# Two spectral layers and two convolution layers on one core: when the rows of the second layer are made, how its norms are split, and which buffers it loads into

## The chip, the cores and the metric

One core of a Trainium2 chip runs the whole program in one launch. The metric is device time in microseconds (us): the median of the runs shown. The engines are named as in the profile: PE is TensorE (matrix products), PEld its weight loads, DVE is VectorE, ACT is ScalarE, POOL is GpSimd, SP is SyncE, which here only issues DMAs.

## The reference, cut to what matters

The input x has 2048 rows (the sequence) of 576 elements (the hidden dimension), in float32. Four sublayers follow each other, each added to its input; the third and fourth repeat the first two.

```python
x = x + A(layernorm(x))      # layer 1
x = x + B(layernorm(x), ...)
x = x + A(layernorm(x))      # layer 2
x = x + B(layernorm(x), ...)

# A: real part of a DFT over the hidden dimension and over the sequence
a = einsum("bsd,ed->bse", x, dft_hid_re)
b = einsum("bsd,ed->bse", x, dft_hid_im)
y = einsum("ts,bse->bte", dft_seq_re, a) - einsum("ts,bse->bte", dft_seq_im, b)

# B: a gate; everything beside x comes from k, v and the kernels, not from x
kv = causal_conv4(k, shift_k) * v
y = causal_long_conv(kv, ssm_k) + kv * ssm_D      # by FFT, length 2 * 2048
return x * y
```

The long convolution does not depend on x. The kernel computes it once and uses it for both B sublayers.

## The kernel before, in words

**Products.** Every float32 matrix is cut in two parts of reduced precision, "high" and "low" (`split`, lines 84 to 86: ACT copies the high part, DVE subtracts it to get the low part), and a product is three matmuls: high·high, high·low, low·high. A matmul moves 512 columns in the sequence products and 288 columns in all others.

**Layer 1 and the first block of layer 2** are run by `layer` (lines 277 to 315). The 2048 output positions are four blocks `tb`; for each block and each of the cosine and the sine matrix (`g`) there are 16 steps `k`, one for each chunk of 128 positions. In a step PE multiplies row chunk X[k] (the normalized row, kept in `xs`, both parts) by one tile of the sequence matrix `c_mat` into four PSUM banks `s` and one bank `rm` for the last 64 columns: 14 matmuls of 512 columns. The tile of `c_mat` (256 KB) is loaded two steps ahead into one of `CRAW` raw tiles and split into one of three `cs` tiles (`load_c`, lines 186 to 193). After 16 steps the banks are moved into the tile `u` (`evac_u`, `evac_r`). Layer 1 has 128 steps (n = 0 to 127), the first block of layer 2 has 32. The generator yields twice in a step, and the code around it puts other work there.

**The hidden DFT** of a finished block (`hidden`, lines 252 to 266) works on `u` and on the matrix W: 27 matmuls of 288 columns make one half of one row chunk, called a piece here. `finish(pending, n)` emits n pieces. In layer 1 pieces of one block are spread over steps of the next; the last block of layer 1 is finished in the first steps of layer 2, one piece a step, so that row 12 of layer 1's output is complete after step 2 of layer 2, row 13 after step 4, row 14 after step 6 and row 15 after step 8 (line 830).

**W** is loaded by `load_w` (lines 200 to 225) in nine chunks through the ring of raw tiles `wl`: three chunks after each of the steps 41, 42 and 43 (lines 608 to 610). The `wl` tiles lie over tiles that the branch used before: the first four over `so` (results on their way to memory), the next two over `v`, the last over `tmp`.

**The branch** (the long convolution, `branch`, lines 324 to 522) is a generator. Its first part (16-point and 128-point transforms of kv and the kernel, "f1") takes 33 calls of `next(br)` and ends at step 40 (F1_END). Its second part ("mid" and "i2") lays out its tiles, loads the constants `mc` on POOL's queue and its first two inputs from the DRAM tensor `t` (lines 495 and 496), splits them and goes on in units of `mid_forward`, `mid_inverse` and `i2_products`, paced by `spent` from step 44 (W_END + 1) on (lines 611 to 620). In the kernel before, all of that begins with the first paced call at step 44, after the nine loads of W.

**Norms.** `normed` (lines 165 to 169) and `normed_x` (lines 532 to 542) normalize a row chunk: statistics, then a power by POOL (`L162`, `L539`), then one small DVE operation and one ACT pass that use it. In layer 1 `get_x0` (line 551) does this for row j up to XLEAD = 3 steps ahead of its use, and `to_x` (lines 171 to 176) puts both parts into `xs`.

**Rows of layer 2.** `get_x1` (lines 562 to 572) loads a row chunk `xa` of layer 1's output and the gate `yb`, makes the gated row (`gated`, lines 524 to 530), stores it (`xb`, line 569), normalizes it, stores that (`y`, line 571) and puts it into `xs`. Its tiles are six `xa`, six `yb` and two `xj`. In the kernel before it is called for rows 0 to 11 after each of the steps 113 to 124 of layer 1 (PREP = 113, lines 625 to 630), and for rows 12 to 15 by `layer` itself, at the start of steps 9 to 12 of layer 2, three steps ahead of use (lines 285 to 287).

**The other three blocks of layer 2** are computed by one level of Strassen's scheme (`strassen`, lines 768 to 824): seven products m in the order 5, 1, 6, 2, 7, 3, 4, each in four steps `kp` of two halves. A step has 12 matmuls of 512 columns, and 16 in the products 5, 1, 2 and 4, which also fill a bank for the last 64 columns. `load_step` (lines 716 to 730) loads 512 KB of `c_mat` a tile: two tiles a step for products 5 and 7, one for 1, 2 and 4, none for 6 and 3. Raw tiles come from the ring `cw` (three tiles, one in `flts`, two in `ph`) or `csum`. `ahead(n + 4, ...)` emits loads four steps ahead. The last-columns bank of the sine side is `rm`, that of the cosine side one of the three banks `b` (`bank()`); `store_r` (lines 697 to 702) moves it out at the end of products 2 and 4. The tiles are laid out at step 14 of layer 2 (STATIC, lines 831 to 844): `save`, `both` and `post` share the rest of `ph`.

**Order.** The code emits work in the order written; the framework then gives each engine and each DMA queue one fixed order, by a priority that follows the order of emission and by its own estimate of when an instruction can start, so an engine's order is not exactly that of the code. On the chip each engine and each queue runs its order in sequence.

Of the kernel before, what the change touches and what calls it, by code (L numbers as in the profile page):

```python
# [10 lines left out]
F32 = mybir.dt.float32  # L11
# [13 lines left out]
EPS = 1e-5  # L25
ASTAT = 8
XLEAD = 3
K_FIRST = 2
F1_16 = 4
F1_END = 40  # L30
# [28 lines left out]
def fnet_h3_kernel(ctx: ExitStack, tc: tile.TileContext, x, c_mat, w_re, w_im, k_pad, v, shift_k,  # L59
# [51 lines left out]
    def lay(t, at, *sizes):  # L111

        for name, words, n in sizes:
            ring.setdefault(name, Ring()).tiles.extend(t[:, at + i * words:at + (i + 1) * words] for i in range(n))
            at += n * words
        assert at <= t.shape[1], (at, t.shape, sizes)
        return at
# [46 lines left out]

    def normed(src, y):
        mv, rs, nb = norm_stats(src)
        nc.vector.tensor_scalar(nb, mv[:, 0:1], rs, -1.0, op0=OP.mult, op1=OP.mult)
        nc.scalar.activation(y, src, AF.Identity, bias=nb, scale=rs)
        return y

    def to_x(y, j):
        t = xs[:, j, :]
# [27 lines left out]
    W = []  # L200

    def load_w():
        lay(flts, SC_AT + CRAW * NT, ("wl", D, 7))
        wg = region_a(FR, "w").rearrange("p (k n) -> p k n", k=9)
        for ch in range(9):
            w = two(wg[:, ch])
            raw = ring["wl"]()
            if ch < 8:
                nc.sync.dma_start(raw, (w_re if ch < 4 else w_im)[(ch % 4) * P:(ch % 4 + 1) * P, :])
            else:  # L210
                nc.sync.dma_start(raw[:REM], w_re[NC * P:, :])
                nc.sync.dma_start(raw[REM:], w_im[NC * P:, :])
            for lo, hi, sg in ((0, P, 1 if ch < 4 else -1),) if ch < 8 else ((0, REM, 1), (REM, P, -1)):
                if sg > 0:
                    split(w[lo:hi, 0, :], w[lo:hi, 1, :], raw[lo:hi])
                else:
                    nc.scalar.activation(w[lo:hi, 0, :], raw[lo:hi], AF.Copy, scale=-1.0)
                    nc.vector.scalar_tensor_tensor(w[lo:hi, 1, :], raw[lo:hi], -1.0,
                                                   w[lo:hi, 0, :].bitcast(F32), op0=OP.mult,
                                                   op1=OP.subtract)  # L220
            W.append(w)
            yield
        for ch in range(9):
            load_after(w_d[ch], wg[:, ch].bitcast(F32))
            yield
# [51 lines left out]
    def layer(get_x, xres, done, pending, blocks=TB):  # L277
        steps = [(g, tb, k) for tb in range(blocks) for g in range(2) for k in range(J)]
        for n, (g, tb, k) in enumerate(steps):
            for i in range(2):  # L280
                if n == 0 and steps[i] not in CT:
                    load_c(steps[i])
            if n + 2 < len(steps):
                load_c(steps[n + 2])
            for i in range(XLEAD + 1):
                if n + i < J:
                    get_x(n + i)
            if k == 0:
                ps = list(acc4)
                ps.append(psp.tile([P, NT], F32, tag="rm", name="rm"))  # L290
            c = CT.pop(steps[n])
            first, last = k == 0, k == J - 1
            if last and g == 0:
                finish(pending, 99)
            for dc in range(NC):
                xh = X[k][:, dc * P:(dc + 1) * P]
                xl = X[k][:, D + REM + dc * P:D + REM + (dc + 1) * P]
                mm(ps[dc], xh, c[0], first, False)
                mm(ps[dc], xh, c[1], False, False)
                mm(ps[dc], xl, c[0], False, last)  # L300
                if dc == NC // 2 - 1:
                    yield n, False
                if last:
                    (evac_u if blocks == TB else save_u)(g, ps, dc)
            xr = X[k][:, NC * P:D + REM]
            mm(ps[NC], xr, c[0], first, False)
            mm(ps[NC], xr, c[1], False, last)
            if last and blocks < TB:
                store_r(tb, g, ps[NC])
            elif last:  # L310
                evac_r(g, ps)
                if g == 1:
                    us = dict(U)
                    pending.extend([us, tb, jj, xres, done] for jj in range(TB))
            yield n, True
# [8 lines left out]
    def branch():  # L324
# [170 lines left out]

        load_feed(0)
        load_feed(1)
        split_feed(0)
        for i, (kind, hf, q) in enumerate(feeds):
            df, fc = halves.pop(i)  # L500
# [31 lines left out]
    def normed_x(src, y, junk):  # L532
        m = ring["stat"]()
        sm, sv, rs, nb = (m[:, i:i + 1] for i in range(4))
        nc.scalar.activation(junk, src, AF.Copy, accum_out=sm)
        nc.vector.tensor_scalar(sm, sm, -1.0 / D, None, op0=OP.mult)
        nc.scalar.activation(junk, src, AF.Square, bias=sm, accum_out=sv)
        nc.vector.tensor_scalar(sv, sv, 1.0 / D, EPS, op0=OP.mult, op1=OP.add)
        pows.append(nc.gpsimd.tensor_tensor(rs, sv, mhalf, OP.pow).ins)  # L539
        nc.vector.tensor_tensor(nb, sm, rs, OP.mult)  # L540
        nc.scalar.activation(y, src, AF.Identity, bias=nb, scale=rs)
        return y

    XL = {}

    def load_x(j):
        if j < J:
            XL[j] = ring["x"]()
            nc.sync.dma_start(XL[j], x[:, j, :])

    def get_x0(j):
        if X[j] is None:
            load_x(j + 2)
            src = XL.pop(j)
            X[j] = to_x(normed_x(src, src, ring["junk"]()) if j >= ASTAT else normed(src, src), j)

    def done0(j, xa):
        nc.sync.dma_start(xa_d[j], xa)
# [3 lines left out]
    def get_x1(j):  # L562
        if j in ready:
            return
        ready.add(j)
        xa = ring["xa"]()
        load_after(xa, xa_d[j])
        xb = gated(xa, j, True)
        nc.sync.dma_start(xb_d[j], xb)
        y = normed_x(xb, xa, ring["xj"]())  # L570
        stored.append(nc.sync.dma_start(y_d[j // 2][:, j % 2, :], y).ins)
        X[j] = to_x(y, j)

# [26 lines left out]
    for n, whole in layer(get_x0, lambda j: x[:, j, :], done0, pending):  # L600
        if whole and n <= F1_END:
            want = K_FIRST + (F1_16 * n // 16 if n <= 16 else F1_16 + (32 - K_FIRST - F1_16) * (n - 16) // (F1_END - 16))
            while used < want:
                next(br)
                used += 1
            if n == F1_END:
                next(br)
        if whole and F1_END < n <= W_END:
            for _ in range(3):
                next(wl, 0)  # L610
        if n > W_END:
            if whole and pieces(n):
                finish(pending, 1)
            m = n - W_END - 1
            if m + 1 < len(paced):
                done_by = paced[m] + (paced[m + 1] - paced[m] if whole else STEP * 3 / 7)
            else:
                done_by = total
            while spent < work * done_by / total:
                spent += next(br, work)  # L620
        if not whole:
            continue
        if n >= W_SAVE and n % 2 == 0:
            next(wl, 0)
        m = n - PREP
        if m == 0:
            lay(flts, SC_AT + CRAW * NT + 2 * D, ("xa", D, 2), ("yb", D, 2))
            lay(region_b(F32, "gate"), 0, ("xa", D, 4), ("yb", D, 4), ("xj", D, 2))
        if 0 <= m < TB * (TB - 1):
            get_x1(m)  # L630
    T, R, t7 = {}, {}, []

    def t_slot(m, kp):
# [134 lines left out]
    def strassen():  # L768
        acc, rem = {}, {}
        for n, (tb, m, kp) in enumerate(steps):  # L770
            if kp == 0:
                acc[m] = pair(m, acc)
                if m in (5, 1):
                    g = REMS[m][0]
                    rem[g] = psp.tile([P, NT], F32, tag="rm", name="rm") if g else bank()
            for i in range(2):
                ahead(n + 4, 2 * n + i + CSB)
                c = cs.pop(2 * n + i)
# [48 lines left out]
    for n, whole in layer(get_x1, lambda j: xb_d[j], done1, pending, 1):  # L827
        if not whole:
            continue
        finish(pending, 1)  # L830
        if n == STATIC:
            anchor.append(stored[-1])
            t7.append(region_a(FR, "t7"))
            ph = region_b(F32, "ph")
            fresh("craw", "rems")
            lay(flts, SC_AT, ("rems", 2 * REM, 2), ("csum", WIDE, 4), ("cw", WIDE, 1))
            at = lay(ph, 0, ("cw", WIDE, 2))
            lay(ph, at, ("save", NT, 8))
            lay(ph, at, ("both", WIDE, 2), ("post", WIDE, 2))
            ring["craw"].tiles.extend(c[:, :NT] for c in ring["cw"].tiles)  # L840
            old = ring.pop("cs")
            free, *held = (old() for _ in range(3))
            lay(t7[0], 7 * WIDE + 16 * REM, ("cs", WIDE, 2))
            ring["cs"].tiles.extend([free, *held])
# [104 lines left out]
```

## Time and profile before

| | |
|---|---|
| median of 3 runs (lowest to highest) | 1245.86 us (1243.02 to 1246.0) |
| profiled execution, device time | 1238.42 us |
| span of that execution (first to last instruction) | 1236.6 us |
| mean granted TensorE clock | 0.992 of full speed |
| PE busy | 1192.3 us (96%), 6320 matmuls |
| DVE busy / ACT busy / POOL busy | 847.0 / 657.1 / 80.9 us |
| DMA traffic | 261.97 MB, mean 212 GB/s |

A row of the windows view gives a stretch, its length, then for each engine the busy time and the number of instructions in it, the granted clock of TensorE, the busy share of the DMA engines and GB/s. A row of the chain of waits gives start, length and what the chain ran through. A row of the timeline gives start, length, engine, line, operation, output<-inputs, shapes, a count, and in brackets how long the engine had been idle and what ended that. A row of the groups view gives line, engine, operation, tiles, shapes and count, then busy time and mean duration in ns, then idle time before. PE's busy time uses modelled ends of the matmuls. All times inside the span are counted from its start.

### The profile page before, as it was taken

Reading aid. Unit: us, or ns where it says so; the run is one execution under the profiler, and the core shown is the slowest. Engines: PE = TensorE matmul, PEld = TensorE weight load, DVE = VectorE, ACT = ScalarE, POOL = GpSimd, SP = SyncE. Lnnn points to the kernel's source line nnn. Section 1 sums busy time; section 2 is a strip of 40 time slices with the busy share of each in tenths; the row PEclk is TensorE's granted clock in tenths of the full one; section 3 lists DMA queues with packets and bytes.
Section 4 is the critical chain, followed back from the end, with each engine's and each line's share of the span. In section 5 each row is a group of like instructions: output and inputs, shape, how many; then the busy total and the mean of one; then the engine's idle time right before and its main releaser. Section 6 shows DMA issues by size and latency. Waiting matters only on the chain.

```text
span 1236.6 us, 18361 instructions
## 1 busy us (share of the span) xinstructions
PE 1192.3 (96%) x6320; PEld 1033.2 (84%) x6320; DVE 847.0 (68%) x1559; ACT 657.1 (53%) x1315; POOL 80.9 (7%) x116
## 2 busy tenths in 40 slices
PE   7999998999999999999999998999999999999997
PEld 6778887987888888898987797888778787789997
DVE  7999983759786677775368615676676667674674
ACT  7955665659776667765457614544344344460220
POOL 1210000000000000001113102000000000000111
PEclk9999999999999999999999999999999999999999
DMA  8989988536656656566968635882673678776631
GB/s 303 306 256 305 292 266 254 183 109 172 193 192 209 195 180 192 181 190 198 327 222 271 228 95 189 267 280 77 191 268 95 180 254 266 230 266 222 207 127 40
DMA packets 145968, 261.97 MB, mean 212 GB/s; under 512 B 15825, under 2 KB 44497, under 8 KB 145874
## 3 DMA queue, kind: packets, MB, share of 16 engines
q1 hardware_dynamic: 102674, 205.73, 52.2%
q10 hardware_dynamic: 36288, 42.48, 9.9%
q0 software_dynamic: 6912, 12.59, 4.0%
q8 instruction: 50, 0.82, 0.3%
q14 instruction: 44, 0.36, 0.1%
HBM read 194.09 MB, written 66.65 MB: 211 GB/s over the span
## 4 chain that ended last, share of the span: by engine, by line
PE 70%; DVE 10%; DMA 10%; ACT 5%; issue 3%; POOL 1%; SPq 0%; ACTq 0%; POOLq 0%; DVEq 0%
PE s L68 36%; PE bk L68 28%; PE rm L68 6%; DMA ph<-in_c_mat 2%; DMA flts<-in_c_mat 2%; DVE mats L86 2%; ACT mats L85 1%; POOL flts L539 1%; DVE ph L725 1%; DMA gate<-xa 1%; DVE mats L176 1%; DMA xb<-gate 1%; DMA flts<-t 1%; POOL flts L162 1%; DVE f1f L383 1%
## 5 line engine op out<-in xcount | busy, mean ns | idle before, releaser
L68 PE MATMUL s<-mats 128*128 128x512 f32 x2094 | 532.3, 395 | 13.5 <-DVE u L86 6.5
L68 PEld LDWEIGHTS s<-mats 128*128 128x128 f32 x2094 | 388.0, 190 | 89.4 <-DVE u L86 7.6
L85 ACT ACTIVATE mats<-flts 128x512 fp32r<-128x512 f32 x209 | 130.9, 627 | 147.8 <-PE rm L68 101.3
L86 DVE TENSOR_TENSOR mats<-flts,mats 128x512 fp32r<-128x512 f32 x209 | 143.3, 688 | 67.3 <-ACT mats L85 65.0
L68 PE MATMUL bk<-mid 128*128 128x288 f32 x768 | 128.2, 301 | 7.3 <-ACT mid L85 4.1
L68 PEld LDWEIGHTS bk<-mid 128*128 128x128 f32 x768 | 113.3, 188 | 25.1 <-ACT mid L85 8.2
L86 DVE TENSOR_TENSOR mid<-flts,mid 128x576 fp32r<-128x576 f32 (+1 forms) x160 | 100.4, 637 | 33.9 <-ACT mid L85 30.6
L68 PEld LDWEIGHTS bk<-w,u 128*128 128x128 f32 x864 | 119.2, 190 | 3.7 <-ACT flts L452 1.3
L68 PE MATMUL bk<-w,u 128*128 128x288 f32 x864 | 121.3, 297 | 0.9 <-ACT flts L452 0.9
L85 ACT ACTIVATE mid<-flts 128x576 fp32r<-128x576 f32 (+1 forms) x160 | 92.5, 586 | 37.2 <-DVE flts L441 29.6
L68 PE MATMUL rm<-mats 128*128 128x512 f32 x338 | 105.5, 392 | 2.6 <-DVE flts L701 1.7
L68 PEld LDWEIGHTS rm<-mats 128*128 128x128 f32 x338 | 63.5, 189 | 17.0 <-DVE flts L701 2.1
L162 POOL TENSOR_TENSOR flts<-flts 128x1 f32<-128x1 f32 x40 | 36.8, 921 | 559.6 <-DVE flts L161 554.9
L264 DVE TENSOR_TENSOR flts<-flts,bk 128x288 f32<-128x288 f32 x48 | 21.7, 452 | 69.0 <-PE bk L68 68.8
L68 PE MATMUL bk<-f1r 128*128 128x288 f32 x384 | 60.6, 300 | 7.7 <-ACT f1r L85 6.4
L68 PEld LDWEIGHTS bk<-f1r 128*128 128x128 f32 x384 | 57.1, 192 | 12.2 <-ACT f1r L85 6.4
L68 PE MATMUL s<-t,mats 128*128 128x512 f32 x258 | 64.3, 389 | 0.0
L68 PEld LDWEIGHTS s<-t,mats 128*128 128x128 f32 x258 | 48.4, 188 | 10.1
L68 PE MATMUL bk<-mats 128*128 128x288 f32 (+1 forms) x340 | 56.8, 309 | 0.0
L398 ACT ACTIVATE flts<-bk 128x288 f32<-128x288 f32 x128 | 48.5, 410 | 14.7 <-PE bk L68 12.6
L438 DVE TENSOR_TENSOR flts<-bk,flts 128x288 f32<-128x288 f32 x64 | 29.1, 455 | 32.7 <-ACT flts L434 32.4
L68 PEld LDWEIGHTS bk<-mats 128*128 128x128 f32 x340 | 48.8, 188 | 2.0
(148 smaller groups left out, 1559.8 us busy)
## 6 DMA issues: line engine op xcount, KB each, us to landing
flts<-in_c_mat SPq DMA_DIRECT2D x150, 256.0 KB, 3.5
ph<-in_c_mat SPq DMA_DIRECT2D x48, 512.0 KB, 3.9
t<-flts ACTq DMA_DIRECT2D x64, 288.0 KB, 4.5
flts<-t SPq DMA_DIRECT2D x64, 288.0 KB, 3.4
flts<-in_c_mat SPq DMA_DIRECT2D x36, 512.0 KB, 5.0
vd<-flts ACTq DMA_DIRECT2D x64, 144.0 KB, 3.0
flts<-vd SPq DMA_DIRECT2D x32, 288.0 KB, 4.1
mid<-in_i2c POOLq DMA_DIRECT2D x32, 256.0 KB, 4.4
```

The source lines that it names most:

```text
L68: nc.tensor.matmul(ps, lhsT, rhs, start=first, stop=last, skip_group_check=more)
L85: nc.scalar.activation(h, src, AF.Copy)
L86: nc.vector.tensor_tensor(l, src, h.bitcast(F32), OP.subtract)
L162: pows.append(nc.gpsimd.tensor_tensor(rs, ve, mhalf, OP.pow).ins)
L176: nc.vector.tensor_tensor(t[:, D + REM:], y[:, :NC * P], h[:, :NC * P], OP.subtract)
L264: nc.vector.tensor_tensor(r[:, cs], r[:, cs], ps[:, :HD], OP.add)
L383: nc.vector.tensor_tensor(r, r, tmp, OP.add)
L398: nc.scalar.activation(so[:, c, :], ps[:, :HD], AF.Copy)
L438: nc.vector.tensor_tensor(p1, px[:, :HD], p1, OP.mult)
L539: pows.append(nc.gpsimd.tensor_tensor(rs, sv, mhalf, OP.pow).ins)
L725: nc.vector.tensor_tensor(src, src, r, OP.add)
```

## The change

1. Rows of layer 2: during layer 1, `get_x1` is called for rows 0 to 7 only, after every second step from 113 to 127. Rows 8 to 15 are made in layer 2, after the steps 0, 1, 2, 3, 4, 5, 7 and 9 (`ROWS`). In the first block of layer 2, `layer` no longer looks three steps ahead (by then each row has been asked for).
2. The loads of the branch's second part: `load_w` gets four raw tiles (over `so`) in place of seven, and the second part of the branch yields once right after its first two loads. It is called for that after step 42, behind the sixth chunk of W; its paced calls begin at step 44 as before.
3. Norms in two steps: `normed` and `normed_x` yield after the power. In layer 1 the statistics and the power of row j + 1 are emitted before the rest of row j (`stats0`). In layer 2 both halves of a norm still follow each other.
4. Strassen's raw tiles: the ring `cw` has four tiles in place of three, `save` six in place of eight, `post` one in place of two.
5. Banks: the last-columns bank of both sides is one of the three banks `b`; `rm` is no longer used there.

```diff
+ROWS = (0, 1, 2, 3, 4, 5, 7, 9)
...
     def normed(src, y):
         mv, rs, nb = norm_stats(src)
+        yield
         nc.vector.tensor_scalar(nb, mv[:, 0:1], rs, -1.0, op0=OP.mult, op1=OP.mult)
         nc.scalar.activation(y, src, AF.Identity, bias=nb, scale=rs)
-        return y
...
-        lay(flts, SC_AT + CRAW * NT, ("wl", D, 7))
+        lay(flts, SC_AT + CRAW * NT, ("wl", D, 4))
...
-            for i in range(XLEAD + 1):
+            for i in range(XLEAD + 1 if blocks == TB else 1):
                 if n + i < J:
                     get_x(n + i)
...
         load_feed(0)
         load_feed(1)
+        yield 0
         split_feed(0)
...
         pows.append(nc.gpsimd.tensor_tensor(rs, sv, mhalf, OP.pow).ins)
+        yield
         nc.vector.tensor_tensor(nb, sm, rs, OP.mult)
         nc.scalar.activation(y, src, AF.Identity, bias=nb, scale=rs)
-        return y
-
-    XL = {}
+
+    XL, LN = {}, {}
...
+    def stats0(j):
+        if j < J and j not in LN:
+            src = XL.pop(j)
+            LN[j] = src, normed_x(src, src, ring["junk"]()) if j >= ASTAT else normed(src, src)
+            next(LN[j][1])
+
     def get_x0(j):
         if X[j] is None:
             load_x(j + 2)
-            src = XL.pop(j)
-            X[j] = to_x(normed_x(src, src, ring["junk"]()) if j >= ASTAT else normed(src, src), j)
+            stats0(j)
+            if j > 0:
+                stats0(j + 1)
+            src, ln = LN[j]
+            next(ln, 0)
+            X[j] = to_x(src, j)
...
-        y = normed_x(xb, xa, ring["xj"]())
+        y = xa
+        for _ in normed_x(xb, y, ring["xj"]()):
+            pass
...
             for _ in range(3):
                 next(wl, 0)
+            if n == W_END - 1:
+                next(br)
...
-        if 0 <= m < TB * (TB - 1):
-            get_x1(m)
+        if m >= 0 and m % 2 == 0:
+            get_x1(m // 2)
...
-                    rem[g] = psp.tile([P, NT], F32, tag="rm", name="rm") if g else bank()
+                    rem[g] = bank()
...
         finish(pending, 1)
+        if n in ROWS:
+            get_x1(J // 2 + ROWS.index(n))
...
-            at = lay(ph, 0, ("cw", WIDE, 2))
-            lay(ph, at, ("save", NT, 8))
-            lay(ph, at, ("both", WIDE, 2), ("post", WIDE, 2))
+            at = lay(ph, 0, ("cw", WIDE, 3))
+            lay(ph, at, ("save", NT, 6))
+            lay(ph, at, ("both", WIDE, 2), ("post", WIDE, 1))
```

## The prediction

> **What bounds the kernel now.** First the page: which engine fills the span.
>
> ```profile
> PE 1192.3 (96%) x6320; PEld 1033.2 (84%) x6320; DVE 847.0 (68%) x1559; ACT 657.1 (53%) x1315; POOL 80.9 (7%) x116
> ```
>
> PE is the bound, and no part of the change takes a matmul away. So the only time to be had is the 1236.6 - 1192.3 = 44.3 us in which PE has nothing to do, and what the granted clock adds to it. The chain of waits gives what PE costs at its peak:
>
> ```profile
> 731.37 3.60 PE bk L68 x27
> 734.97 2.74 PE s L68 x12
> ```
>
> 2.74 / 12 = 0.228 us for a matmul of 512 columns; a step of layer 1 is 14 of them, 3.2 us. The 27 of 288 columns above it are a hidden piece, 3.6 us. Next the windows view, to place the idle time (length less PE's busy time):
>
> ```profile
> 40.00:60.00 20.00, 18.65 (x89) 15.27 (x88) 17.86 (x42) 17.84 (x38) 4.32 (x5) 1.00 0.87 302
> 60.00:80.00 20.00, 17.48 (x83) 14.14 (x82) 18.31 (x34) 13.09 (x27) 3.36 (x5) 1.00 0.80 230
> 200.00:220.00 20.00, 16.65 (x76) 14.21 (x76) 9.75 (x15) 10.69 (x20) 1.59 (x3) 0.91 0.92 276
> 216.53:219.95 3.42, 3.42 (x17) 3.42 (x16) 2.17 (x5) 2.89 (x7) 0.00 (x0) 0.50 0.71 218
> 660.00:702.00 42.00, 37.93 (x169) 31.11 (x168) 35.80 (x99) 33.23 (x66) 12.96 (x15) 0.92 0.83 280
> 702.00:764.00 62.00, 62.00 (x346) 55.16 (x345) 20.39 (x46) 13.66 (x24) 4.12 (x5) 1.00 0.39 127
> 764.00:780.00 16.00, 11.68 (x43) 8.88 (x42) 8.32 (x22) 9.03 (x18) 2.09 (x3) 0.89 0.64 213
> 885.00:900.00 15.00, 13.90 (x58) 10.35 (x57) 10.47 (x15) 7.70 (x14) 0.00 (x0) 1.00 0.78 252
> 979.00:994.00 15.00, 13.82 (x57) 10.28 (x56) 10.44 (x15) 7.48 (x13) 0.00 (x0) 1.00 0.83 251
> 1074.00:1090.00 16.00, 13.81 (x57) 10.92 (x55) 9.93 (x14) 7.13 (x13) 0.00 (x0) 0.89 0.77 226
> ```
>
> Two things are to be seen. The idle time stands at few places, and each part of the change is aimed at one. And behind some waits the clock is granted at 0.50 for 3.42 us (the row at 216.53): PE is "busy" there and does half the work, so such a wait costs 1.7 us more than its length. A clock of 0.92 over 42 us is two such stretches, 0.89 over 16 us is one, 0.91 over 20 us is one.
>
> The Trainium skill, "TensorE: Matmul & The Clock Gate", Part 1, has this halving come after about one idle window of 3.4 us, with windows that run freely. The trace halves the clock after shorter waits too (1074 to 1090 has 2.19 us idle in all), and 60 to 80, with 2.52 us idle, stays at 1.00. By the page's length alone, closing the short waits would return no clock time.
>
> **Rows of layer 2.** DVE's groups between 640 and 776 us, and PE's two longest waits from 640 to 780 (us in total, times, longest):
>
> ```profile
> L86 DVE TENSOR_TENSOR mats<-flts,mats 128x512 fp32r<-128x512 f32 x30 | 20.6, 687 | 23.4 <-ACT mats L85 23.0 <-DMA yb<-flts 0.4
> L159 DVE BATCH_NORM_STATS2 flts<-gate 128x6 f32<-128x288 f32 x20 | 8.8, 449 | 1.3 <-DMA gate<-xa 1.3
> L529 DVE SCALAR_TENSOR_TENSOR gate<-gate,flts 128x576 f32<-128x576 f32 x10 | 8.1, 811 | 0.4 <-POOL flts L162 0.4
> L528 DVE SCALAR_TENSOR_TENSOR gate<-gate,flts 128x576 f32<-128x576 f32 x10 | 8.1, 810 | 0.1
> L176 DVE TENSOR_TENSOR mats<-gate,mats 128x512 fp32r<-128x512 f32 x10 | 6.8, 684 | 0.0
> ...
> L538 DVE TENSOR_SCALAR flts<-flts 128x1 f32<-128x1 f32 x16 | 2.3, 145 | 4.7 <-ACT gate L537 4.7
> ```
>
> ```profile
> PE s L68 <- ACT mats L173: 3.9, 1, 3.9
> PE s L68 <- DVE u L86: 2.5, 1, 2.5
> ```
>
> A row costs DVE 2 x 0.449 + 0.811 + 0.810 + 0.684 + 4 x 0.145 = 3.8 us at least, and each step one split of 0.69: 4.5 us of DVE work in a step of 3.2 us. Twelve such steps in a row cannot be kept up; splits come late, and the chain of waits shows SP's queue behind them too, stores of rows that wait for DVE with the next tile of `c_mat` behind them:
>
> ```profile
> 663.28 5.06 DMA xb<-gate
> 668.72 3.50 DMA xb<-gate
> 672.66 5.04 DMA flts<-in_c_mat
> ```
>
> Then rows 12 to 15 are asked for only three steps (9.6 us) ahead, and PE waits 3.9 us for one of them (L173). In between, from 702 to 764, DVE is busy 20.39 of 62 us, since a hidden piece makes each step 6.8 us long. The change gives layer 1 eight rows in 16 steps, 3.8 + 1.4 = 5.2 us of DVE in 6.4 us, and puts the other eight where steps are long: 4.5 us in 6.8. Rows 12 to 15 are then asked for six to eight steps ahead (row 15 after step 9, 19 us before step 15) instead of three. No instruction is added; rows, stores and loads move. The cover of the eight moved rows is DVE's 41.6 idle us from 702 to 764, against 8 x 3.8 = 30 us; without that cover each would cost PE what its step lacks, as the twelve rows do now.
>
> To be had: 660 to 702, 4.07 us idle and 2 x 1.7 of clock; 764 to 780, 4.32 and 1.7: 13.5 us. A block boundary with DVE still 81% loaded can keep a wait for `u`; I leave 1.5 us there and take **12**. Bounds: 6.0 (only 764 to 780 goes) to 13.5.
>
> **Strassen's tiles and banks.** The chain before 896:
>
> ```profile
> 876.06 3.56 DMA ph<-in_c_mat
> 881.00 3.78 DMA flts<-in_c_mat
> 886.12 3.44 DMA ph<-in_c_mat
> 890.84 4.03 DMA ph<-in_c_mat
> ```
>
> Four loads one behind the other, each issued only when a tile of the ring is free, about 5 us apart. Product 7 takes two tiles a step of 2.74 us, so with three tiles the fourth load waits for the first to be added and split. With four, two steps' pairs are in flight together, and the chain loses one link of 5 us; the waits that it ends in are 1.10, 1.18 and 2.19 us with 1.7 of clock, 6.2 us. I take **5** (bounds 0 to 6.2). One tile `post` less: its uses are four steps or more apart, 4 x 2.74 = 11 us, and a transfer of this size takes 3.4 to 4.0 us above, so nothing waits; `save` is used four at a time, 16 steps apart. The banks, by PE's waits from 836 to 1115:
>
> ```profile
> PE s L68 <- ACT mats L85: 3.6, 4, 2.2
> PE rm L68 <- DVE flts L701: 2.2, 2, 1.7
> ```
>
> PE waits twice for `store_r` (L701) of product 4 before it may write `rm` for the next product 5. With three banks in turn there is no such wait: **2.2 us** (bounds 0 to 2.2).
>
> **Norms in two steps.** From 40 to 80 DVE is busy 17.9 to 18.3 us of 20; its short L540 waits for POOL, and ACT for L540:
>
> ```profile
> 46.02 0.87 ACT L541 ACTIVATE early<-early,flts 128x576 f32<-128x576 f32 x1 [1.29 <-DVE flts L540]
> ```
>
> ACT stands 1.29 us there, and the move of a bank of PE's stands behind ACT. With the power one row ahead, other work fills that time. PE's idle time from 40 to 80 is 1.35 + 2.52 = 3.9 us, the second part at a block boundary; I take **2**. From below: a row's statistics stand ahead of the first steps' splits, 2 x 0.449 and small ones, so it can cost 1.3 us.
>
> **Loads among W's.** The chain ahead of PE's wait between 200 and 220 (the first input of the second part), and DVE's last split of W:
>
> ```profile
> 210.75 0.58 SPq L212
> 211.34 0.04 issue
> 211.38 3.82 DMA flts<-t
> ```
>
> ```profile
> 214.99 0.76 DVE L218 SCALAR_TENSOR_TENSOR w<-flts,w 64x576 fp32r<-64x576 f32 x1
> ```
>
> The loads from `t` go out behind the last of W (L212) and land at 215.2; moved ahead of three chunks they land some 3 us earlier. But W itself is split only at 215.75, and the hidden piece that follows needs all nine chunks. With four raw tiles, chunks 5 to 9 each wait until a tile has been split, and the three that were loaded long ahead into `v` and `tmp` (DMA share is 0.92 here already) join the queue: a round of load (3.8 us, as that of `t`) and a split (0.76 us on DVE, an estimate of the same on ACT) is 5.3 us, so W is done up to 5.3 us later. A piece needs its last chunk only 3.2 us after its start. So the gain of up to 3.35 + 1.7 = 5.05 us is mostly eaten: I take **0.5** (bounds -5.3 to 5.05).
>
> **Sum:** 12 + 5 + 2.2 + 2 + 0.5 = 21.7 us. The profiled execution (1236.6 us of span, 1238.42 in all) would come to 1216.7. The runs shown stand 7.4 us above it (median 1245.86); measured like them, 1245.86 - 21.7 = **1224**.
>
> **The rivals.**
>
> 1. *W is late (12%).* The four tiles cost the full 5.3 us at 200 to 220 instead of gaining 0.5: 1230. For it: W's last split ends at 215.75 now, half a microsecond after the input of the second part has landed. Against: matmuls of steps 45 and 46 can go first.
> 2. *The clock does not come back (10%).* Short waits remain where long ones stood, and three of the four half-clock stretches that I count as gone stay: 3 x 1.7 less, 1229. For it: 2.19 us is enough to halve it. The limit of the page of the Trainium skill named above would give this time too.
> 3. *Only Strassen gains (12%).* Rows that no longer disturb one stretch delay another, and the start gains nothing; 7.2 us alone: 1239. For it: from 40 to 80 DVE is near 90%, and an engine so full has work of some kind late whichever order it takes. Against: DVE's 41 idle us after 702.
> 4. *SP's queue behind the moved rows: slower (8%).* Row 12 takes from the issue of `xa` at 739.74 to that of its `y` store at 751.64, 11.9 us:
>
> ```profile
> 739.74 0.42 SPq L146 DMA_DIRECT2D flts<-xa  x1
> ...
> 751.64 0.32 SPq L571 DMA_DIRECT2D y<-flts  x1
> ```
>
> If SP issues each next tile of `c_mat` only behind a row's `y` store, a step takes 11.9 us instead of 6.8 in eight steps: 8 x 5.1 = 41 us lost against 21.7 gained, 1265. It decides from a row's time on the queue of 6.8 + 21.7 / 8 = 9.5 us. Against: that row stands in 702 to 764, where PE is busy 62.00 of 62.00 us, so tiles of `c_mat` pass it.
> 5. *All of it (8%).* Every bound at its best: 3.9 + 5.05 + 13.5 + 8.4 = 30.9 us, 1215.
>
> **How the numbers follow.** My own forecast, 1224, holds 50%. The range reaches from a little below all of it to Strassen alone, **1213 to 1240**, and leaves out the slower rival and some of the third. What a measurement can tell from no change is about 0.3%, 3.7 us: faster means below 1242. Faster 0.88 (the forecast, rivals 1, 2 and 5, most of 3), within 0.3% 0.04 (the rest of 3), slower 0.08 (rival 4).
>
> **What would show it.** PE at 660 to 700 and at the twelfth step of layer 2 without idle time and with the clock at 1.00; DVE near 80% from 702 to 764; no PE wait for L701; in products 7 two loads in flight at once; fewer DVE waits for L539. Wrong would be: PE waiting for L217 or L218 or W's loads near 215, tiles of `c_mat` late in the first ten steps of layer 2, or a new wait at the block boundaries.

## The result and the profile after

| | before | changed |
|---|---|---|
| median, first measurement | 1244.44 us (1242.9 to 1246.0, 4 runs) | 1230.51 us (1225.59 to 1231.17, 4 runs) |
| ratio, 95% interval | | 0.9879 (0.9849 to 0.991) |
| median, measured again | 1241.58 us (17 runs) | 1227.85 us (6 runs), ratio 0.9902 (0.9881 to 0.9923) |
| profiled execution | 1238.42 us, span 1236.6 | 1229.91 us, span 1228.0 |

So the change makes the kernel 12 to 15 us faster, by the two ratios; 21.7 were forecast. The profile of the changed kernel, with the same stretches as before (two are moved to where the waits now stand: 215 to 221.83 and 764 to 790). Lines have moved by one to sixteen; L87 is the old L86, L537 the old L535, L544 the old L541, L717 the old L701. First the page's line of the engines:

```profile
PE 1189.8 (97%) x6320; PEld 1032.7 (84%) x6320; DVE 849.3 (69%) x1559; ACT 657.3 (54%) x1315; POOL 85.5 (7%) x116
```

The windows view of the changed kernel (length, then busy time and count of PE, PEld, DVE, ACT and POOL, granted clock, DMA share, GB/s):

```profile
40.00:60.00 20.00, 18.04 (x84) 14.38 (x83) 19.15 (x46) 19.73 (x42) 6.36 (x5) 1.00 0.95 332
60.00:80.00 20.00, 17.79 (x77) 14.17 (x76) 18.31 (x34) 12.32 (x24) 3.39 (x5) 0.91 0.76 224
200.00:220.00 20.00, 16.59 (x77) 14.23 (x77) 8.60 (x13) 10.05 (x18) 1.58 (x3) 0.88 0.93 291
215.00:221.83 6.83, 5.38 (x22) 5.39 (x23) 4.95 (x8) 5.14 (x10) 0.00 (x0) 0.50 0.91 285
660.00:702.00 42.00, 37.70 (x161) 30.98 (x160) 31.50 (x81) 26.41 (x51) 8.17 (x11) 0.92 0.77 257
702.00:764.00 62.00, 62.00 (x355) 55.23 (x355) 36.02 (x98) 26.87 (x52) 12.93 (x15) 1.00 0.58 190
764.00:790.00 26.00, 22.80 (x92) 17.71 (x91) 15.39 (x30) 14.76 (x28) 0.55 (x1) 0.93 0.83 262
885.00:900.00 15.00, 14.96 (x66) 12.07 (x65) 10.66 (x16) 8.13 (x14) 0.00 (x0) 1.00 0.82 270
979.00:994.00 15.00, 15.00 (x67) 12.21 (x66) 10.34 (x16) 7.03 (x13) 0.00 (x0) 1.00 0.88 304
1074.00:1090.00 16.00, 16.00 (x70) 12.79 (x70) 13.66 (x22) 10.26 (x19) 0.00 (x0) 1.00 1.01 366
```

Three readings. The Strassen stretches (the last three rows) are full: the idle time of 1.10, 1.18 and 2.19 us is 0.04, 0 and 0, and the clock stays at 1.00. From 702 to 764 DVE went from 20.39 to 36.02 us busy and PE lost nothing there, as forecast. But 660 to 702 is as bad as it was: 4.30 us idle (4.07 before) and a clock of 0.92, and 764 to 790 still has 3.20 us idle (4.32 before) and one half-clock stretch. From 40 to 80, where the norms were to gain, PE's idle time is 4.17 us (3.87 before), and a half-clock stretch is there (0.91 in 60 to 80) that the trace before does not have. PE's waits from 640 to 800 us in the changed kernel (us in total, times, longest):

```profile
PE s L69 <- DVE u L87: 4.2, 1, 4.2
PE rm L69 <- DVE flts L717: 2.5, 1, 2.5
PE s L69 <- ACT ph L710: 0.7, 1, 0.7
```

The waits for rows (L173, 3.9 us) and for late splits are gone. In their place PE waits at two block boundaries: 4.2 us at the end of layer 1, where it was 2.5, and 2.5 us in the middle of layer 2's first block, where there was none.

**The first boundary, by ACT's timeline of the changed kernel.** PE's last twelve matmuls into the four banks `s` start at 685.77 and take 3.28 us, three to a bank, the first bank first. A bank is free for the next step when ACT and DVE have moved it into `u`:

```profile
685.77 3.28 PE L69 MATMUL s<-mats 128*128 128x512 f32 x12
```

```profile
690.18 0.68 ACT L537 ACTIVATE gate<-flts 128x576 f32<-128x576 f32 x1 [1.16 <-DVE flts L531]
690.77 0.19 ACT L537 ACTIVATION_READ_ACCUMULATOR gate<-flts 128x1 f32 x1
691.07 0.87 ACT L544 ACTIVATE flts<-flts 128x576 f32<-128x576 f32 x1
691.84 0.61 ACT L86 ACTIVATE mats<-flts 128x512 fp32r<-128x512 f32 x1
692.36 0.57 ACT L86 ACTIVATE u<-s 128x512 fp32r<-128x512 f32 x1
```

```profile
693.84 0.80 PE L69 MATMUL s<-mats 128*128 128x512 f32 x1 [4.21 <-DVE u L87]
```

ACT moves the bank only at 692.36, because the passes of the last rows (L537, L544) and one split stand ahead of it in its order, and the first of these waits 1.16 us for DVE. DVE is 75% busy in that stretch: an engine that is no bound on average holds PE by what stands ahead in its order.

**The second boundary, by DVE's timeline of the changed kernel:**

```profile
779.01 0.69 DVE L677 TENSOR_TENSOR flts<-flts 128x512 f32<-128x512 f32 x1 [1.47 <-DMA flts<-y]
779.74 0.69 DVE L678 TENSOR_TENSOR flts<-flts 128x512 f32<-128x512 f32 x1
780.47 0.69 DVE L681 TENSOR_TENSOR flts<-flts 128x512 f32<-128x512 f32 x1
782.16 0.29 DVE L672 TENSOR_TENSOR flts<-flts 128x128 f32<-128x128 f32 x1 [1.00 <-DMA flts<-y]
782.55 0.69 DVE L686 TENSOR_TENSOR flts<-flts 128x512 f32<-128x512 f32 x1
783.16 0.67 DVE L717 TENSOR_TENSOR flts<-flts,rm 64x512 f32<-64x512 f32 x1
```

The additions that build Strassen's operands (`build`, L672 to L686) stand in DVE's order ahead of `store_r` (L717), and two of them wait for loads of `y`. PE may not write `rm` before L717. The trace before has such additions ahead of the same move too (L661 and L662, the first behind a wait for `y`), and the move starts only 0.8 us earlier there. But PE came later:

```profile
782.34 0.67 DVE L701 TENSOR_TENSOR flts<-flts,rm 64x512 f32<-64x512 f32 x1
784.59 0.61 PE L68 MATMUL rm<-mats 128*128 128x512 f32 x2
```

In the changed kernel PE is ready for its first matmul into `rm` at 783.88 - 2.49 = 781.39, 3.2 us earlier than before. The wait for row 12 had covered this one.

**The loads among W's, by SP's timeline, SP's waits and the chain of waits of the changed kernel:**

```profile
211.97 0.33 SPq L210 DMA_DIRECT2D flts<-in_w_im  x1
212.35 0.90 SPq L147 DMA_DIRECT2D flts<-t  x2
```

```profile
SPq L210 <- DMA t<-flts: 6.4, 3, 5.4
SPq L210 <- DVE w L87: 4.5, 3, 1.5
```

```profile
211.19 0.77 DVE w L87
211.97 0.33 SPq L210
212.35 3.25 DMA flts<-t
```

The loads from `t` go out at 212.35; they went out at 211.38 before. They are ahead of the last chunks of W, but right behind a chunk (L210 at 211.97) that SP could issue only when DVE had split the raw tile that it takes. PE's wait for the input of the second part is 3.41 us (3.35 before). W itself is split last at 222.48 + 0.75 = 223.2 instead of 215.75:

```profile
222.48 0.75 DVE L219 SCALAR_TENSOR_TENSOR w<-flts,w 64x576 fp32r<-64x576 f32 x1 [0.39 <-ACT w L218]
```

### The profile page after: what moved, and what is told of

Its sections match the earlier page's. It is cut to its first block, busy times and chain, and to the rows that moved or that the text cites. A ratio compares the mean times of both kernels' runs of the same rounds, so it can differ in the third digit from the quotient of the medians.

```text
span 1228.0 us, 18406 instructions
## 1 busy us (share of the span) xinstructions
PE 1189.8 (97%) x6320; PEld 1032.7 (84%) x6320; DVE 849.3 (69%) x1559; ACT 657.3 (54%) x1315; POOL 85.5 (7%) x116
## 4 chain that ended last, share of the span: by engine, by line
PE 76%; DVE 7%; DMA 7%; ACT 5%; issue 3%; POOL 1%; SPq 0%; ACTq 0%; POOLq 0%; DVEq 0%
PE s L69 41%; PE bk L69 31%; PE rm L69 4%; DVE mats L87 1%; DMA flts<-in_c_mat 1%; DMA f1f<-in_k_pad 1%; DMA gate<-xa 1%; POOL flts L541 1%; ACT mats L86 1%; DMA flts<-in_w_re 1%; ACT flts L436 1%; DVE u L87 1%; DVE flts L160 1%; DMA flts<-t 1%; ACT mid L86 0%
## 5 line engine op out<-in xcount | busy, mean ns | idle before, releaser
L86 ACT ACTIVATE mats<-flts 128x512 fp32r<-128x512 f32 x202 | 126.2, 626 | 106.0 <-PE rm L69 53.8
L87 DVE TENSOR_TENSOR mats<-flts,mats 128x512 fp32r<-128x512 f32 x202 | 138.3, 687 | 53.4 <-ACT mats L86 51.9
L87 DVE TENSOR_TENSOR mid<-flts,mid 128x576 fp32r<-128x576 f32 (+1 forms) x160 | 100.5, 637 | 34.9 <-ACT mid L86 29.4
L86 ACT ACTIVATE mid<-flts 128x576 fp32r<-128x576 f32 (+1 forms) x160 | 92.4, 586 | 37.6 <-DVE flts L442 27.8
L69 PE MATMUL rm<-mats 128*128 128x512 f32 x308 | 96.1, 391 | 3.3 <-DVE flts L717 2.5
L69 PEld LDWEIGHTS rm<-mats 128*128 128x128 f32 x308 | 57.5, 188 | 16.3 <-DVE flts L717 2.9
L69 PE MATMUL bk<-mats 128*128 128x288 f32 (+1 forms) x370 | 66.0, 316 | 0.0
L265 DVE TENSOR_TENSOR flts<-flts,bk 128x288 f32<-128x288 f32 x48 | 21.6, 451 | 59.3 <-PE bk L69 59.2
L69 PE MATMUL bk<-mats,t 128*128 128x288 f32 (+1 forms) x362 | 57.4, 302 | 0.0
L69 PEld LDWEIGHTS bk<-mats 128*128 128x128 f32 x370 | 54.4, 188 | 3.2
L399 ACT ACTIVATE flts<-bk 128x288 f32<-128x288 f32 x128 | 48.3, 408 | 14.2 <-PE bk L69 12.2
```

The source lines that it names most:

```text
L69: nc.tensor.matmul(ps, lhsT, rhs, start=first, stop=last, skip_group_check=more)
L86: nc.scalar.activation(h, src, AF.Copy)
L87: nc.vector.tensor_tensor(l, src, h.bitcast(F32), OP.subtract)
L265: nc.vector.tensor_tensor(r[:, cs], r[:, cs], ps[:, :HD], OP.add)
L399: nc.scalar.activation(so[:, c, :], ps[:, :HD], AF.Copy)
```

## The experiments

Theory A, from these traces: the rows' gain is given back at the two boundaries, Strassen's parts are worth what they show, the other two parts little or nothing. Rival B: each part is worth its term of the forecast, and the shortfall comes from elsewhere or from the parts meeting each other. Each part was put into the kernel before by itself, in one series on one chip (before: 1240.62 us median, 29 runs).

### Each part alone

**p1_rows**, part 1 alone:

```diff
-            for i in range(XLEAD + 1):
+            for i in range(XLEAD + 1 if blocks == TB else 1):
...
-        if 0 <= m < TB * (TB - 1):
-            get_x1(m)
+        if m >= 0 and m % 2 == 0:
+            get_x1(m // 2)
...
+        if n in ROWS:
+            get_x1(J // 2 + ROWS.index(n))
```

> The rows of layer 2 alone (part 1), everything else as before. Theory A (the gain of this part is given back at two block boundaries, inside this part): the waits of 3.9 us at 771 and the half clock at 670 and 773 go, but PE waits about 4 us for u near 690 and about 2 to 3 us for store_r near 780, each with half clock behind it; in all 0 to 3 us faster than before. Rival B (the part is worth what was predicted, and the shortfall of the whole change comes from the other parts or from their interplay): 10 to 14 us faster, no PE wait over 1.5 us between 640 and 800.

Measured: 1237.0 us median (12 runs), ratio 0.9966 (0.9953 to 0.998), 4.2 us faster (2.5 to 5.8). Its longest PE waits from 640 to 800 us:

```profile
PE s L69 <- DVE u L87: 4.2, 1, 4.2
PE rm L69 <- DVE flts L702: 2.0, 1, 2.0
PE s L69 <- ACT ph L695: 0.5, 1, 0.5
```

The same two boundary waits as in the whole change, without any of the other parts. B falls for this part; A has the mechanism, and its bound of 3 us lies inside the interval but under the median.

**p45_tiles_banks**, parts 4 and 5 alone:

```diff
-            at = lay(ph, 0, ("cw", WIDE, 2))
-            lay(ph, at, ("save", NT, 8))
-            lay(ph, at, ("both", WIDE, 2), ("post", WIDE, 2))
+            at = lay(ph, 0, ("cw", WIDE, 3))
+            lay(ph, at, ("save", NT, 6))
+            lay(ph, at, ("both", WIDE, 2), ("post", WIDE, 1))
...
-                    rem[g] = psp.tile([P, NT], F32, tag="rm", name="rm") if g else bank()
+                    rem[g] = bank()
```

> Four raw tiles and the idle banks alone (parts 4 and 5). Theory A: all of Strassen's waits go, 10 to 12 us faster than before, since the traces of before and after differ by that between 860 us and the end. Rival B: 7 us, as predicted, the rest of the change in that stretch being owed to rows that are ready earlier.

Measured: 1232.69 us median (6 runs), ratio 0.9931 (0.991 to 0.9952), 8.6 us faster (6.0 to 11.2). No PE wait is left from 836 to 1115 us. The interval holds the 7 us of the forecast and part of A's 10 to 12; it needs no help from the rows.

**p5_banks**, part 5 alone (one line of the diff above), in a later series (before: 1241.58 us):

> The idle banks alone (part 5): no PE wait for store_r of product 4. Theory E: 2 to 3 us faster than before, the waits of 0.5 and 1.7 us and no more, so that the tiles (part 4) are worth the other 5 to 6 us of the two. Rival F: under 1 us, since PE would wait next for the load behind which store_r stands in DVE's order, so that nearly all of the two parts' 8.6 us is the fourth tile's.

Measured: 1238.51 us median (12 runs), ratio 0.9976 (0.9961 to 0.9991), 3.0 us faster (1.1 to 4.8). What is left of PE's waits from 836 to 1115 us begins with

```profile
PE s L68 <- ACT mats L85: 3.1, 3, 1.7
```

and has no L701 any more; that wait, for the tiles, was 3.6. Theory E: banks 3.0, and so by difference 5.6 us for the fourth tile, which was not run by itself (the two figures are of different series, each give or take 2 to 3 us).

**p2_w**, part 2 alone:

```diff
-        lay(flts, SC_AT + CRAW * NT, ("wl", D, 7))
+        lay(flts, SC_AT + CRAW * NT, ("wl", D, 4))
...
         load_feed(1)
+        yield 0
...
                 next(wl, 0)
+            if n == W_END - 1:
+                next(br)
```

> The first loads of the second part among W's, with four raw tiles (part 2) alone. Theory A: the loads from t still go out near 212, since SP's queue holds them behind a chunk of W that waits for a raw tile, and W is split 5 to 7 us later: 1 to 3 us slower than before. Rival B: the loads go out near 208 and PE's wait of 3.35 us shrinks by 0.5 to 3 us: as much faster.

Measured: 1241.7 us median (12 runs), ratio 1.0007 (0.9989 to 1.0024), 0.9 us slower (1.4 faster to 3.0 slower). In its timeline the loads from `t` go out at 212.90 and W's last split starts at 223.46:

```profile
212.90 0.90 SPq L146 DMA_DIRECT2D flts<-t  x2
```

```profile
223.46 0.75 DVE L218 SCALAR_TENSOR_TENSOR w<-flts,w 64x576 fp32r<-64x576 f32 x1 [0.39 <-ACT w L217]
```

A's picture; its price can't be told from nothing. PE's wait for the input of the second part is 3.88 us here, against 3.35 before.

**p3_norms**, part 3 alone (the two `yield`s, `stats0` and `get_x0` of the diff above):

> Norms in two steps alone (part 3). Theory A: no gain in the first 80 us, because DVE is the bound there and the waits for POOL move to other instructions: within 2 us of before. Rival B: 2 us faster, with DVE's waits for L539 (its number here differs) gone and PE's waits from 40 to 80 us shorter by 2 us.

Measured: 1239.0 us median (12 runs), ratio 0.9981 (0.9965 to 0.9998), 2.4 us faster (0.2 to 4.3). DVE's waits for POOL in the first 80 us, before:

```profile
DVE flts L540 <- POOL flts L539: 2.6, 6, 0.4
DVE flts L167 <- POOL flts L162: 1.8, 4, 0.7
```

and with part 3:

```profile
DVE flts L541 <- POOL flts L539: 2.1, 5, 0.4
DVE flts L168 <- POOL flts L162: 1.6, 3, 0.7
```

The time is near that of B, but its mechanism is not seen. The waits for POOL shrink from 4.4 to 3.7 us, and PE's idle time from 40 to 80 us goes from 3.9 to 3.6; over the whole of the first 80 us it is 11.6, against 11.2 before. So A's trace, no gain in the first 80 us, is what shows, and where the 2.4 us come from stays open.

The four together: 4.2 + 8.6 - 0.9 + 2.4 = 14.3 us, against 12.2 and 15.1 for the whole change. The sum is uncertain by about 4 us, from the four intervals. Within that the parts add up; no meeting of parts is needed.

### The two boundaries

A second theory follows, C: each of the two waits comes from an engine's order, and a change that takes other work from in front of the move takes the wait. Its rival D: the wait belongs to the boundary, or goes to the next consumer. These ran as changes to the changed kernel, against before at 1241.09 us (11 runs).

**x_6rows**, six rows in layer 1 and ten in layer 2:

```diff
-ROWS = (0, 1, 2, 3, 4, 5, 7, 9)
+ROWS = tuple(range(10))
...
-        if m >= 0 and m % 2 == 0:
+        if 0 <= m < 12 and m % 2 == 0:
...
-            get_x1(J // 2 + ROWS.index(n))
+            get_x1(6 + ROWS.index(n))
```

> The changed kernel, with six rows instead of eight made in layer 1 (after steps 113, 115 ... 123) and ten in layer 2 (after steps 0 to 9). Theory C (the wait near 690 is ACT's order: the passes of the last two rows stand ahead of the moves of the banks s into u): the wait of 4.4 us goes to under 1 us and the two half-clock windows behind it with it: 4 to 7 us faster than the changed kernel, that is 19 to 22 us faster than before. Rival D (the wait is the block boundary's own, five banks through two engines): the wait stays at 3 us or more, and the time is that of the changed kernel within 2 us.

Measured: 1231.07 us median (6 runs), ratio 0.9926 (0.9907 to 0.9944), 9.2 us faster than before. Its windows, its longest PE waits from 640 to 800 us and ACT's move of the banks:

```profile
660.00:702.00 42.00, 39.21 (x180) 31.73 (x179) 28.93 (x70) 21.81 (x42) 5.91 (x9) 1.00 0.69 224
702.00:764.00 62.00, 58.58 (x333) 51.33 (x332) 38.71 (x108) 32.09 (x62) 14.45 (x18) 1.00 0.61 211
764.00:790.00 26.00, 21.79 (x94) 17.11 (x93) 14.94 (x29) 14.54 (x27) 0.55 (x1) 1.00 0.78 251
```

```profile
PE rm L69 <- DVE flts L717: 2.9, 1, 2.9
PE s L69 <- DVE u L87: 2.4, 2, 1.5
PE bk L69 <- DVE flts L265: 2.1, 3, 0.9
PE bk L69 <- DVE flts L538: 1.3, 1, 1.3
```

```profile
689.48 2.04 ACT L86 ACTIVATE u<-s 128x512 fp32r<-128x512 f32 x4
```

Both theories have half. (The two waits that the expectations call 4.4 and 2.7 us are the 4.21 and 2.49 us shown above.) ACT begins to move the banks at 689.48 instead of 692.36, with no pass of a row in the 4 us before it; what still stands ahead of the move is a split that waits for a load of `c_mat` until 688.95. The wait for `u` falls from 4.2 us to two of 1.5 and 0.9, which is not under the 1 us of C, and the clock from 660 to 702 is 1.00 instead of 0.92, as C says. The run takes the last rows away from ACT and from DVE at once, so it does not tell ACT's order from DVE's work; no run changes the order alone. But 702 to 764, which had no idle time, now has 3.42 us: with ten rows there, the additions that free the banks of the hidden pieces (L265) come late in DVE's order. The gain goes to the next consumer, as D says, and the time is not the 19 to 22 us faster than before that C gave.

**x_bank**, a bank `b` instead of `rm` for the second half of layer 2's first block:

```diff
-                ps.append(psp.tile([P, NT], F32, tag="rm", name="rm"))
+                ps.append(psp.tile([P, NT], F32, tag="rm", name="rm") if g == 0 or blocks == TB else bank())
```

> The changed kernel, with the last-columns bank of the second half of layer 2's first block taken from the banks b instead of rm. Theory C (the wait near 781 is for store_r, which stands in DVE's order behind additions that wait for loads of y): the wait of 2.7 us and its half-clock window go, 2 to 4.5 us faster than the changed kernel. Rival D (the same lateness of DVE meets the next consumer, a tile of c_mat split late or the banks s): the wait moves by a few matmuls and the time is that of the changed kernel within 1.5 us.

Measured: 1225.36 us median (4 runs), ratio 0.988 (0.9858 to 0.9901), 14.9 us faster than before. Since the changed kernel was not in that series, both were run in a third one:

> The changed kernel itself, on the same chip as the next three, so that they can be compared with it. All theories: 13 to 17 us faster than before, as the sum of its parts measured alone (14.2 us) says.

> The changed kernel with a bank b for the second half of layer 2's first block, beside the changed kernel. Theory C: 2 to 4.5 us faster than the changed kernel, for the wait of 2.7 us and the half-clock window behind it, which are gone from its trace. Rival D: within 1.5 us of it, since the clock's window falls elsewhere in other executions and the wait was covered in part.

Measured: the changed kernel 1227.85 us (6 runs), ratio 0.9902 (0.9881 to 0.9923); with the bank 1224.67 us (6 runs), ratio 0.9866 (0.9843 to 0.989). That is 3 us by the medians. The two intervals overlap a little, but five of the six runs with the bank are faster than the fastest of the changed kernel. In the trace of the second the wait is gone and nothing has taken its place; its waits from 640 to 800 us and its window:

```profile
PE s L69 <- DVE u L87: 4.2, 1, 4.2
PE s L69 <- ACT ph L710: 0.8, 1, 0.8
```

```profile
764.00:790.00 26.00, 25.12 (x110) 20.16 (x109) 15.80 (x31) 14.86 (x28) 0.55 (x1) 1.00 0.80 259
```

Idle time there falls from 3.20 to 0.88 us and the clock is 1.00 instead of 0.93. C holds for this boundary.

### Without part 2, and the best version

**after_no_p2**, the changed kernel with part 2 undone, and **x_all**, with part 2 undone, six rows and the bank, in the series of x_6rows:

> The changed kernel with part 2 undone (seven raw tiles for W, the second part's loads behind W's). Theory C (part 2 costs a little, as alone: W is split 5 to 7 us later and the loads from t are no earlier): 0 to 3 us faster than the changed kernel. Rival D (beside the other parts it gains the 0.5 us of the prediction or more): 0 to 3 us slower than the changed kernel.

> The three together: six rows in layer 1, the bank b in layer 2's first block, part 2 undone. Theory C: 7 to 14 us faster than the changed kernel, 22 to 29 us faster than before, with no PE wait over 1.5 us between 600 us and the end. Rival D: the waits move, and it is within 4 us of the changed kernel.

Measured: 1228.37 us (6 runs), ratio 0.9904 (0.9885 to 0.9923), and 1227.76 us (6 runs), ratio 0.9894 (0.9874 to 0.9913). Without part 2 the changed kernel's time stays where it was (0.9879 and 0.9902 with it), so part 2 has no effect that shows. x_all is 13 us faster than before, not the 22 to 29 of C. By the times the six rows take back what the bank gives. The trace of x_all does not show where: its idle time from 640 to 800 us is 5.6 us, and its longest PE wait there 1.5 us. That stays open.

**x_bank_no_p2**, the bank and eight rows, part 2 undone, in the third series:

> The same with part 2 undone as well. Theory C: 0 to 2 us faster than the one with part 2 (alone, part 2 cost 0.9 us, with an interval from 1.4 us faster to 3 us slower). Rival D: slower by 0 to 3 us, since the changed kernel without part 2 was 0.24% slower against before than the changed kernel in its first measurement.

Measured: 1223.06 us median (4 runs), ratio 0.9855 (0.9832 to 0.9879), 18.0 us faster than before: the best of the versions measured. Its interval lies below that of the changed kernel in the same series (0.9881 to 0.9923): it beats both kernels. Between it and the bank alone (0.9866) nothing can be told.

## Why the prediction was right, and where it was too high

- **The direction and the range held:** 1230.5 us, inside 1213 to 1240, and so did the gain at Strassen, which is most of what was gained. The forecast itself was 6.5 us too low in time; the gain was 12 to 15 us instead of 21.7.
- **Strassen's tiles and banks, 5 + 2.2 us:** 8.6 us together (6.0 to 11.2), 3.0 for the banks and by difference 5.6 for the tile. The reading of the chain (loads one behind the other, about 5 us apart, each behind a raw tile) was right, and no new wait came.
- **Rows of layer 2, 12 us:** the step that failed. Measured 4.2 us (2.5 to 5.8), below the bound of 6.0 that was given. The waits for rows and for late splits went as said, and from 702 to 764 PE has no idle time, as said. But DVE is busy 36.02 of 62 us there, 58%, not near 80%: 36.02 - 20.39 = 15.6 us is the work of four rows, not of eight. Rows 12 to 15 were made in layer 2 before, too, so only rows 8 to 11 moved there. What failed is "a block boundary with DVE still 81% loaded can keep a wait for `u`; I leave 1.5 us there". The load of DVE was lower than that, 75%, and the wait was 4.2 us. Behind it the clock is at half until 699.75, for 5.9 us of PE's work, 3.0 us more: about 7.2. A share of busy time says nothing of where the move of a bank stands in ACT's order. And the second boundary (2.5 us and 1.7 of clock) was not seen, because before the change PE arrived there late by the wait for row 12; taking that wait away laid it bare. The account closes in the trace of the rows alone: from 660 to 790 its idle time is 4.21 + 0.18 + 2.60 = 7.0 us, with two half-clock stretches, 3.4, together 10.4 of the 13.5 us that were to be had. The 3.1 us that are left lie within the 2.5 to 5.8 measured.
- **Norms, 2 us:** 2.4 us (0.2 to 4.3) by the times; the reason given, fewer waits for POOL, is hardly in the trace. That the size fits is luck as far as these runs show.
- **Loads among W's, 0.5 us:** 0.9 us slower (1.4 faster to 3.0 slower). The working said that the loads from `t` would land some 3 us earlier; they go out 1 to 1.5 us later, behind a chunk that waits for its raw tile. W is done 7.5 us later, more than the bound of 5.3. PE does not wait for W in either trace; its one wait from 196 to 240 us is that for the input of the second part, 3.35 us before and 3.41 after, so there is neither a gain nor a cost to see.
- **The rivals:** the first two gave 1230 and 1229, very near the measured time, but by other mechanisms. The first (W is late) did not occur, since PE does not wait for W. The second (the clock does not come back) has the count right: of the four half-clock stretches counted as gone, the changed kernel has three, two from 692.92 and one from 785.06, but behind the two boundary waits and not behind short remains of the old ones. The third names what happened to the rows, "rows that no longer disturb one stretch delay another", though they still gained 4.2 us. The fourth (SP's queue, slower) did not occur: tiles of `c_mat` passed the moved rows.
- **The signs:** Strassen's products have no wait for `store_r` any more, as said. The two stretches of the rows were to be without idle time and at a clock of 1.00, and are not. And one sign of being wrong came: a new wait at a boundary, for `store_r` in layer 2's first block.

## What to carry to other kernels

When work is moved off a full stretch, look at the next place where the bound engine must wait for a buffer to be emptied, and read there which instructions stand ahead of the emptying in that engine's order: its share of busy time doesn't tell. A wait that is taken away can lay bare one that it had covered, as row 12's did here. Look also at what a load that is put earlier in the code still has ahead of it on its queue: here that was a chunk that waited for a raw tile, and with fewer raw tiles the load went out no earlier.

## What the runs showed of the hardware

Behind some of PE's waits the granted clock is halved for 3.41 us, or for twice that. The length of the wait does not decide it alone. The clock was halved behind waits of 1.33 us (trace before, ending at 669.21, with one of 0.27 us just ahead of it), 1.83 us (changed kernel, ending at 74.03) and 2.49 us (changed kernel, ending at 783.88), and not behind waits of 2.44 us (trace before, ending at 74.18) and 2.92 us (x_6rows, ending at 784.79). Behind the same wait of 4.21 us it was at half for 6.83 us in the changed kernel (692.92 to 699.75, the first 0.9 us still in the wait) and for 3.41 us in p1_rows (694.32 to 697.73), so this wait cost 7.2 us in one trace and 5.9 in the other. Two waits of 1.5 and 0.9 us in its place were followed by no half clock in x_6rows and by one stretch in x_all.

The stretches of one execution lie on a grid. In the trace before they begin at 216.53, 670.51, 697.81, 772.91 and 1083.52 us, which are 133, 8, 22 and 91 times 3.413 us apart. So where a wait falls on that grid may decide with its length; what share of a period PE must be idle is not shown here.

The Trainium skill, "TensorE: Matmul & The Clock Gate", Part 1, asks for about one idle window of 3.4 us before the clock is halved; the waits of 1.33, 1.83 and 2.49 us differ from that, and the measurement decides.
